# Stationary K/V, bf16 pairs and whole-head transfers in an attention backward pass with one query row

## The chip, the cores and the metric

The kernel runs on one core of a Trainium2 chip. The metric is device time in microseconds of one execution. Every quoted time is the median over the runs of a kernel; where a single run was taken, this is said. The experiments were run in five sessions, each on another chip; the kernel before was run in each of them on the same chip and stayed between 1480.9 and 1481.6 us (medians), so the experiments can be compared with each other.

Names used below: PE is the matmul engine (TensorE), PEld its weight loads, which overlap with PE, DVE the vector engine, ACT the scalar engine, POOL the engine that issues the loads and SP the one that issues the stores. PEclk is the granted clock of PE, where 1.00 is full speed. A "head" is one of 64 (batch, head) pairs.

## The reference

```python
B, H, Sq, Sk, D = 2, 32, 1, 8192, 128          # all bf16

def _fwd_reference(q, k, v):
    scale = q.shape[-1] ** -0.5
    scores = jnp.einsum("bhqd,bhkd->bhqk", q, k) * scale
    p = _softmax(scores, axis=-1)
    return jnp.einsum("bhqk,bhkd->bhqd", p, v)

def reference(q, k, v, grad_out):
    # ... jax.vjp of the forward ...
    return (out, dq, dk, dv)
```

With one query row, a head needs two passes of products over K and V. The scores `q.K` and `dp = do.V` contract over D. The sums `o = p.V` and `dq = ds.K` contract over the 8192 positions. The gradients `dK = ds x q` and `dV = p x do` are outer products. K and V are 2 MB each for a head, and so are dK and dV. Over all heads that makes 268 MB in and 268 MB out, so the transfers are a bound of their own.

## The kernel before

Per head, cut. The partition axis holds 128 groups of 64 consecutive positions (`NT = 64`), so a tile of K is 128 positions by 128 dimensions.

```python
# loads: four pieces of 512 KB each for K and for V (4 KB runs), from POOL
load_eng.dma_start(out=kt[:], in_=k_v[bh, :, c * lp : (c + 1) * lp, :])

# scores and dp: 16 transposes on PE, eviction by ACT, 16 matmuls of one column
for c in range(nch):                                   # 4 chunks
    for which, (Tn, col) in enumerate(((Kn, qcol), (Vn, docol))):
        tp = ps_tp.tile([P, ch, P], BF16, tag="tp")    # 2 buffers
        for i in range(ch):
            nc.tensor.transpose(tp[:, i, :], Tn(n), ident_bf[:])
        ev = evp.tile([P, ch, P], BF16, tag="ev")
        nc.scalar.copy(out=ev[:], in_=tp[:])
        for i in range(ch):
            nc.tensor.matmul(sdp[:, which, n:n+1], lhsT=ev[:, i, :], rhs=col, start=True, stop=True)

# softmax chain: max, exp (E_f), sums, ds ... on DVE, ACT and PE        [cut]

# o, then dq: p (or ds) stationary with one column, V (or K) moving with 128
for n in range(NT):
    nc.tensor.matmul(acc[:, 0, :], lhsT=E_bf[:, n:n+1], rhs=Vn(n), ...)
for n in range(NT):
    nc.tensor.matmul(acc[:, 1, :], lhsT=dS_bf[:, n:n+1], rhs=Kn(n), ...)
nc.scalar.activation(out=orow[:], in_=acc[:, 0, :], func=ACT.Copy, scale=rl[0:1, :])
nc.scalar.activation(out=qrow[:], in_=acc[:, 1, :], func=ACT.Copy, scale=rls[0:1, :])

# outer products on DVE, bf16 times fp32, 16 tiles at a time, stored by SP (4 KB runs)
nc.vector.tensor_tensor(out=dKc[:], in0=qb_b, in1=dSs[...].to_broadcast([P, oc, D]), op=ALU.mult)
```

## Time and profile before

| | before |
|---|---|
| median of 4 runs | 1481.06 us (1480.61 to 1482.01) |
| mean granted clock of PE | 0.978 |
| one head, median (exponentials to exponentials) | 22.4 us |
| ACT busy + ACT waiting | 981.7 + 481 = 1463 of 1480.5 us |
| DMA, mean over the span | 368 GB/s |

These are lines of the page of the kernel before: the span, the busy time of each engine (with its share of the span and its instructions), and the granted clock in tenths over 40 equal slices.

```profile
span 1480.5 us, 54950 instructions
PE 1285.7 (87%) x24898; PEld 1184.9 (80%) x24898; DVE 1260.1 (85%) x1347; ACT 981.7 (66%) x769; POOL 271.9 (18%) x520
PEclk9999999999999999999999999999999999999997
```

PE and DVE both look full, and DMA, at 368 GB/s, is not far away. Busy shares do not say which of them bounds the kernel. The groups of the same page say more. Their columns are: line, engine, operation, output<-input by name, then by shape, the count; after the bar the busy time and the mean ns of one; after the second bar the idle time just before them and what ended most of it.

```profile
L143 ACT COPY ev<-tp 128x2048 bf16<-128x2048 bf16 x512 | 921.4, 1888 | 47.2 <-PE tp L141 46.6
L268 DVE TENSOR_TENSOR dVc<-dob_all,Pn 128x2048 bf16<-128x2048 bf16 x256 | 585.8, 2288 | 0.1
L141 PE MATMUL tp<-ident_bf,kt 128*128 128x128 bf16 x4096 | 302.4, 224 | 9.1 <-DMA kt<-in_k_dram 9.1
L141 PE MATMUL tp<-ident_bf,vt 128*128 128x128 bf16 x4096 | 301.3, 223 | 1.9 <-DMA vt<-in_v_dram 1.9
L245 ACT ACTIVATE orow<-acc,rl 1x128 bf16<-1x128 f32 x64 | 23.1, 360 | 406.7 <-PE acc L237 406.7
L229 PE MATMUL acc<-vt,E_bf 128*1 128x128 bf16 x4096 | 240.9, 220 | 0.0
```

ACT gives the best account of the time, although it is busy for only 66% of it. Its busy time of 981.7 us, its wait of 406.7 us for the accumulation (the line L245), 46.6 us for transposes and 27.9 us for the softmax sum to 1463 of 1480.5 us. So a head is eight evictions in a row, and then a stop. The timeline shows the stop. Its columns are the start in us, the duration, the engine, and what ran; the bracket is the idle time before it.

```profile
712.08 0.32 ACT L169 ACTIVATE E_f<-sdpw,negm 128x64 f32<-128x64 f32 x1 [0.41 <-DVE negm L164]
...
713.20 3.73 PE L229 MATMUL acc<-vt,E_bf 128*1 128x128 bf16 x64
...
716.18 0.19 DVE L217 CAST dS_bf<-dSu 128x64 bf16<-128x64 f32 x1
...
716.77 3.74 PE L237 MATMUL acc<-kt,dS_bf 128*1 128x128 bf16 x64
...
720.54 0.36 ACT L245 ACTIVATE orow<-acc,rl 1x128 bf16<-1x128 f32 x1 [6.30 <-PE acc L237]
```

PE takes 7.5 us for the two accumulations, and ACT idles 6.30 us before it can copy their result. o needs only the exponentials (E_f at 712.08), so it starts 1.1 us after them, and the making of ds, which ends at 716.37, is hidden behind o's 3.73 us.

### The profile page before, as it was taken

The page shows a single profiled execution, that of the slowest core. Times are in us where ns is not written, and L with a number is a line of the kernel's source. Part 1 is how long each engine was busy: PE and PEld are TensorE (multiplying, and loading weights), DVE is VectorE, ACT ScalarE, POOL GpSimd, SP SyncE. Part 2 cuts the span into 40 slices and gives each one's busy share as a digit, 9 for nine tenths or more (in the row PEclk, how much of TensorE's full clock was granted, in tenths as well). Part 3 has the DMA queues.
Part 4 walks back from the last instruction along what each step waited for, and adds up shares of the span by engine and source line. Part 5 has one row for each costly group of instructions (what it writes and reads, how often), then busy time and mean ns, then how long its engine had stood idle before and what let it go on. Part 6 is the DMA issues. An engine that isn't in the chain of part 4 may idle for free. (4 is left out here: it accounts for less than half of the span.)

```text
span 1480.5 us, 54950 instructions
## 1 busy us (share of the span) xinstructions
PE 1285.7 (87%) x24898; PEld 1184.9 (80%) x24898; DVE 1260.1 (85%) x1347; ACT 981.7 (66%) x769; POOL 271.9 (18%) x520
## 2 busy tenths in 40 slices
PE   5898888898988988988889889888888898888894
PEld 5887887887878878878878888788788788888884
DVE  1988988889889889888898898898888888988988
ACT  5667667667576676676675766766766757667663
POOL 3221211211212212112112112122121121121200
PEclk9999999999999999999999999999999999999997
DMA  9999999999999999999999999999999999999954
GB/s 379 415 385 388 370 373 388 354 382 375 358 392 371 357 393 359 372 383 365 383 385 357 387 367 372 389 361 371 389 358 379 386 360 383 368 373 388 363 241 199
DMA packets 148394, 544.70 MB, mean 368 GB/s; under 512 B 16832, under 2 KB 16832, under 8 KB 147904
## 3 DMA queue, kind: packets, MB, share of 16 engines
q0 software_dynamic: 73728, 268.47, 49.9%
q1 hardware_dynamic: 74064, 268.52, 44.6%
q8 instruction: 194, 3.18, 0.8%
q10 hardware_dynamic: 368, 4.21, 0.7%
q14 instruction: 40, 0.33, 0.1%
HBM read 272.66 MB, written 268.47 MB: 366 GB/s over the span
## 5 line engine op out<-in xcount | busy, mean ns | idle before, releaser
L143 ACT COPY ev<-tp 128x2048 bf16<-128x2048 bf16 x512 | 921.4, 1888 | 47.2 <-PE tp L141 46.6
L268 DVE TENSOR_TENSOR dVc<-dob_all,Pn 128x2048 bf16<-128x2048 bf16 x256 | 585.8, 2288 | 0.1
L260 DVE TENSOR_TENSOR dKc<-qb_all,dSs 128x2048 bf16<-128x2048 bf16 x256 | 575.0, 2290 | 0.0
L146 PEld LDWEIGHTS <-ev 128*128 128x128 bf16 x8192 | 243.0, 96 | 236.2 <-ACT ev L143 226.7
L119 POOL DMA_DIRECT2D vt<-in_v_dram x256 | 135.7, 530 | 962.4 <-PE acc L229 943.4
L141 PE MATMUL tp<-ident_bf,kt 128*128 128x128 bf16 x4096 | 302.4, 224 | 9.1 <-DMA kt<-in_k_dram 9.1
L141 PE MATMUL tp<-ident_bf,vt 128*128 128x128 bf16 x4096 | 301.3, 223 | 1.9 <-DMA vt<-in_v_dram 1.9
L245 ACT ACTIVATE orow<-acc,rl 1x128 bf16<-1x128 f32 x64 | 23.1, 360 | 406.7 <-PE acc L237 406.7
L141 PEld LDWEIGHTS <-kt 128*128 128x128 bf16 x4096 | 250.7, 101 | 9.7 <-DMA kt<-in_k_dram 9.7
L141 PEld LDWEIGHTS <-vt 128*128 128x128 bf16 x4096 | 249.3, 100 | 3.9 <-DMA vt<-in_v_dram 2.1
L229 PE MATMUL acc<-vt,E_bf 128*1 128x128 bf16 x4096 | 240.9, 220 | 0.0
L237 PE MATMUL acc<-kt,dS_bf 128*1 128x128 bf16 x4096 | 239.1, 219 | 0.0
L146 PE MATMUL sdpw<-qT_all,ev 128*128 128x1 bf16 x4096 | 141.5, 164 | 110.1 <-ACT ev L143 110.1
L229 PEld LDWEIGHTS <-E_bf 128*1 128x1 bf16 x4096 | 228.9, 84 | 4.6
L237 PEld LDWEIGHTS <-dS_bf 128*1 128x1 bf16 x4096 | 230.5, 84 | 0.0
L146 PE MATMUL sdpw<-doT_all,ev 128*128 128x1 bf16 x4096 | 141.6, 164 | 55.3 <-ACT ev L143 55.1
L116 POOL DMA_DIRECT2D kt<-in_k_dram x256 | 135.8, 531 | 164.1 <-PE acc L237 143.3
L156 DVE TENSOR_REDUCE mp<-sdpw 128x1 f32<-128x64 f32 x64 | 14.4, 225 | 102.7 <-PE sdpw L146 102.7
L178 DVE CUSTOM_DVE_ANT_0 junk<-E_f,sdpw 128x64 bf16<-128x64 f32 x64 | 14.2, 222 | 30.4 <-ACT E_f L169 30.4
L169 ACT ACTIVATE E_f<-sdpw,negm 128x64 f32<-128x64 f32 x64 | 20.2, 316 | 28.1 <-DVE negm L164 27.9
L160 DVE TENSOR_REDUCE gm<-sdpw 1x1 f32<-1x128 f32 x64 | 17.8, 278 | 23.4 <-PE sdpw L158 23.4
L164 DVE TENSOR_SCALAR negm<-sdpw 128x1 f32<-128x1 f32 x64 | 10.2, 159 | 30.7 <-PE sdpw L162 30.7
(33 smaller groups left out, 261.5 us busy)
## 6 DMA issues: line engine op xcount, KB each, us to landing
kt<-in_k_dram POOLq DMA_DIRECT2D x256, 512.0 KB, 12.1
vt<-in_v_dram POOLq DMA_DIRECT2D x256, 512.0 KB, 7.9
out_dram<-dVc SPq DMA_DIRECT2D x256, 512.0 KB
out_dram<-dKc SPq DMA_DIRECT2D x256, 512.0 KB
qb_all<-in_q_dram ACTq DMA_DIRECT2D x1, 2048.0 KB
dob_all<-in_grad_out_dram ACTq DMA_DIRECT2D x1, 2048.0 KB
out_dram<-orow SPq DMA_DIRECT2D x64, 0.2 KB
out_dram<-qrow SPq DMA_DIRECT2D x64, 0.2 KB
```

Source lines behind the costliest of these rows:

```text
L116: load_eng.dma_start(out=kt[:], in_=k_v[bh, :, c * lp : (c + 1) * lp, :])
L119: load_eng.dma_start(out=vt[:], in_=v_v[bh, :, c * lp : (c + 1) * lp, :])
L141: nc.tensor.transpose(tp[:, i, :], Tn(n), ident_bf[:])
L143: nc.scalar.copy(out=ev[:], in_=tp[:])
L146: nc.tensor.matmul(sdp[:, which, n : n + 1], lhsT=ev[:, i, :], rhs=col, start=True, stop=True,)
L160: nc.vector.reduce_max(out=gm[:], in_=mT, axis=AX.X)
L169: nc.scalar.activation(out=E_f[:], in_=sdp[:, 0, :], func=ACT.Exp, bias=negm[:], scale=scale, accum_out=ld[:, 0:1],)
L229: nc.tensor.matmul(acc[:, 0, :], lhsT=E_bf[:, n : n + 1], rhs=Vn(n), start=(n == 0), stop=(n == NT - 1),)
L237: nc.tensor.matmul(acc[:, 1, :], lhsT=dS_bf[:, n : n + 1], rhs=Kn(n), start=(n == 0), stop=(n == NT - 1),)
L245: nc.scalar.activation(out=orow[:], in_=acc[:, 0, :], func=ACT.Copy, scale=rl[0:1, :])
L260: nc.vector.tensor_tensor(out=dKc[:], in0=qb_b, in1=dSs[:, n0 : n0 + oc].unsqueeze(2).to_broadcast([P, oc, D]), op=ALU.mult,)
L268: nc.vector.tensor_tensor(out=dVc[:], in0=dob_b, in1=Pn[:, n0 : n0 + oc].unsqueeze(2).to_broadcast([P, oc, D]), op=ALU.mult,)
```

## The change

The intent was threefold. First, K and V become the stationary operand for o and dq, with one moving column, so that an accumulating matmul costs as little as a score matmul (0.55 us for 16). Second, p and ds are stored as bf16 in pairs, so that the outer products on DVE have two bf16 inputs. Third, a whole head is loaded and stored in one transfer with runs of 16 KB, and o and dq are collected on chip and written once at the end. The core of the diff:

```diff
-        for c in range(nlp):
-            kt = kvp.tile([P, lp, D], BF16, tag=f"K{c}")
-            load_eng.dma_start(out=kt[:], in_=k_v[bh, :, c * lp : (c + 1) * lp, :])
+        kt = kvp.tile([P, NT, D], BF16, tag="K")
+        load_eng.dma_start(out=kt[:], in_=k_v[bh])
   [V alike; q and do broadcast by a matmul in place of 4 MB of loads]
-        for c in range(nch):
-            for which, (Tn, col) in enumerate(((Kn, qcol), (Vn, docol))):
+        for w, src in enumerate((kt, vt)):
+            for c in range(NCH):
   [...]
-            Pn = work.tile([P, NT], F32, tag="Pn")
-            nc.vector.tensor_scalar(out=Pn[:], in0=E_f[:], scalar1=rl[:], ...)
+            Pn = work.tile([P, NT, 2], BF16, tag="Pn")
+            nc.vector.tensor_scalar(out=Pn[:], in0=E_f[:].unsqueeze(2).to_broadcast([P, NT, 2]), ...)
   [dSs alike]
-        acc = ps_acc.tile([1, 2, P], F32, tag="acc")
-        for n in range(NT):
-            nc.tensor.matmul(acc[:, 0, :], lhsT=E_bf[:, n : n + 1], rhs=Vn(n), ...)
-        for n in range(NT):
-            nc.tensor.matmul(acc[:, 1, :], lhsT=dS_bf[:, n : n + 1], rhs=Kn(n), ...)
-        nc.scalar.activation(out=orow[:], in_=acc[:, 0, :], ...)
-        nc.scalar.activation(out=qrow[:], in_=acc[:, 1, :], ...)
+        acc = ps_acc.tile([P, 2], F32, tag="acc")
+        for w, (src, col, norm) in enumerate(((kt, dS_bf, rls), (vt, E_bf, rl))):
+            for n in range(NT):
+                nc.tensor.matmul(acc[:, w : w + 1], lhsT=src[:, n, :], rhs=col[:, n : n + 1], ...)
+            nc.scalar.activation(out=oT[:, w, bh : bh + 1], in_=acc[:, w : w + 1],
+                                 func=ACT.Copy, scale=norm[:])
   [...]
-            nc.vector.tensor_tensor(out=dKc[:], in0=qb_b, in1=dSs[...].to_broadcast([P, oc, D]), ...)
-            store_eng.dma_start(out=dk_v[bh, :, n0 : n0 + oc, :], in_=dKc[:])
+            ob = outp.tile([P, NT, D], BF16, tag=f"o{w}")
+            for n0 in range(0, NT, OC):
+                nc.vector.tensor_tensor(out=ob[...] as pairs, in0=qb as pairs, in1=sc as pairs, ...)
+            store_eng.dma_start(out=dst[bh], in_=ob[:])
```

## The prediction

> **What bounds the kernel now.** A loop between PE and ACT, not the DMA queues directly. The page gives PE 1285.7 us, DVE 1260.1 us and ACT 981.7 us of a span of 1480.5 us. The waits view shows almost no wait of a compute engine on a load (about 20 us, all at the start) and none of DVE on an output buffer. It shows ACT waiting 406.7 us (64 times, 6.4 us a head) for the accumulation of dq, and PE waiting about 165 us for ACT's evictions. The timeline around 700 us shows why: one head takes about 22.4 us; eight evictions follow each other every 1.77 us (14.2 us), then PE runs 2 x 64 accumulating matmuls (3.73 us each 64) while ACT stands idle, because its next instruction is the copy of o.
>
> DMA stands close behind. One-microsecond windows show 400 to 430 GB/s while PE and ACT evict, and 220 to 340 in the accumulation, where loads wait for buffers; the first 100 us run at 402 to 418. The mean is 368. So about 415 GB/s looks like the ceiling of this mix, already with 4 KB runs.
>
> **What the change does.**
> 1. K and V stationary with one moving column: 16 such pairs took 0.55 us in the score matmuls, so 128 take an estimated 4 us instead of 7.5 us. All of it lies on the loop: minus 3.5 us a head, some 220 us.
> 2. bf16 pairs: the DVE products have two 2-byte inputs with a contiguous innermost pair. The Trainium skill, page "VectorE: DVE Perf Modes", section "The perf-mode tier table", gives 1224 ns for such a bf16 product of 2048 and 2293 ns for fp32; this trace has 2290 ns with the fp32 scalar, which agrees. Estimate: 8 x 1.22 = 9.8 us instead of 18.3 us a head, DVE from 19.7 to about 13.5 us. DVE leaves the near-critical set, and the softmax chain waits less behind a product (about 1 us a head).
> 3. Whole-head transfers: a quarter as many packets, 4.2 MB of broadcast less. Loads now start only when a whole head's buffer is free, and PE starts a head only when 2 MB of K is in. The last store is 2 MB (about 5 us) instead of 512 KB.
>
> **New balance.** Compute loop: 22.4 - 3.5 - 0.5 to 1 = about 18.5 to 19 us a head. DMA: 8.39 MB a head at 415 to 425 GB/s = 19.7 to 20.2 us. So the bound moves to DMA. The page "DMA: Bandwidth & Descriptors", section "Bandwidth", measured 425 GB/s for a 16 MB load; no run here shows 16 KB runs yet, so I take 418. Up to the last load, DMA moves about 126 x 4.19 = 528 MB: 1264 us; plus a start of 3 us and a tail of about 30 us after the last load (V phase 7, softmax 4.5, products 10, last store 7). That is 1297; with some loss between loop and queues I say 1305 us, range 1255 to 1375. Chance of faster by over 2%: 0.95; within 2%: 0.04; slower: 0.01.
>
> **What would show it right.** Accumulating groups of about 30 ns a pair; DVE products near 1.22 us; DVE busy 850 to 900 us; PE busy lower; ACT's wait for acc about halved; new waits of PE on K and V loads of some us a head, spread over the run; mean 405 to 420 GB/s.
>
> **What would make it wrong.** Products staying at 2.29 us (then DVE bounds: about 1450 us). Larger packets lifting DMA above 430 GB/s or lowering it by read/write mixing. PE waiting for whole-head loads long enough for its clock to fall. Compute slower than 20 us a head because ACT still stops for both accumulations.

## The result, and the profile after

| | before | after |
|---|---|---|
| median | 1481.06 us | 1400.01 us (1397.86 to 1402.66, 4 runs) |
| ratio | | 0.9453 (95%: 0.9439 to 0.9466) |
| mean granted clock | 0.978 | 0.705 |
| one head, median | 22.4 us | 21.4 us |
| DMA, mean | 368 GB/s | 386 GB/s |

A ratio is the mean time of one kernel's fast runs over that of the other's of the same rounds, so it is not quite the ratio of the medians. The gain was 81 us where 176 had been forecast, and the time lies above the predicted range.

The same lines of the page, now of the changed kernel:

```profile
span 1399.4 us, 53434 instructions
PE 1238.2 (88%) x24964; PEld 1138.2 (81%) x24964; DVE 745.6 (53%) x1413; ACT 989.3 (71%) x769; POOL 69.8 (5%) x138
PEclk9667677767676667776777676657776777676565
```

DVE lost 515 us of work, and PE lost only 48. The clock row explains the second: PE ran at six or seven tenths of its full clock in the mean of almost every slice. The groups of the changed kernel:

```profile
L117 ACT COPY ev<-tp 128x2048 bf16<-128x2048 bf16 x512 | 934.7, 1869 | 96.5 <-PE tp L115 94.0
L115 PE MATMUL tp<-ident_bf,vt 128*128 128x128 bf16 x4096 | 452.2, 299 | 7.2 <-issue 7.2
L115 PE MATMUL tp<-ident_bf,kt 128*128 128x128 bf16 x4096 | 367.1, 233 | 6.2 <-DMA kt<-in_k_dram 4.2
L228 DVE TENSOR_TENSOR ob<-qb,Pn 128x2048 bf16<-128x2048 bf16 x256 | 306.7, 1220 | 0.2
L214 PE MATMUL acc<-E_bf,vt 128*128 128x1 bf16 x4096 | 125.4, 166 | 32.1 <-issue 31.7
L221 ACT ACTIVATE oT<-acc,rl 128x1 bf16<-128x1 f32 x64 | 16.9, 263 | 178.1 <-PE acc L214 178.1
L214 PE MATMUL acc<-dS_bf,kt 128*128 128x1 bf16 x4096 | 116.0, 164 | 5.5 <-DVE dS_bf L191 2.6
L221 ACT ACTIVATE oT<-acc,rls 128x1 bf16<-128x1 f32 x64 | 16.9, 264 | 96.6 <-PE acc L214 96.6
```

The accumulations fell as predicted, from 240.9 + 239.1 us to 125.4 + 116.0 us (-239 us), and the products fell from 2288 to 1220 ns each. But the same 8192 transposes grew from 302.4 + 301.3 us to 452.2 + 367.1 us (+216 us), although nothing in them was changed. And ACT still stops for the accumulation, now twice a head: 178.1 + 96.6 = 274.7 us, after 406.7 us. Its whole account reads: busy +8, wait for the accumulation -132, wait for transposes +47, wait for the softmax -5. That is -82 us, and the time fell by 81. So the question is why these two waits stayed so long.

These are windows of one microsecond of the changed kernel around one accumulation. The columns after the length are the busy time of PE, PEld, DVE, ACT and POOL with counts, then the granted clock, the busy share of the DMA engines and GB/s.

```profile
713.00:714.00 1.00, 0.98 (x39) 0.92 (x36) 1.00 (x2) 0.00 (x0) 0.00 (x0) 0.63 0.96 410
714.00:715.00 1.00, 1.00 (x34) 1.00 (x32) 1.00 (x2) 0.26 (x1) 0.41 (x1) 0.50 1.08 459
...
723.00:724.00 1.00, 0.90 (x13) 0.73 (x11) 0.00 (x0) 0.95 (x2) 0.00 (x0) 0.75 1.05 442
```

The accumulation starts at 712.34. In the window from 713 to 714 the clock is halved, and it stays at 0.50 for nine microseconds (714 to 723), of which PE is busy for 8.2 us. It is no lack of work for PE that lowers the clock; what does is counted out below, under the width of the moving operand. And this is the timeline of the same stretch:

```profile
708.87 0.31 ACT L143 ACTIVATE E_f<-sdpw,negm 128x64 f32<-128x64 f32 x1 [0.41 <-DVE negm L138]
...
712.34 1.95 PE L214 MATMUL acc<-dS_bf,kt 128*128 128x1 bf16 x64
...
714.33 0.26 ACT L221 ACTIVATE oT<-acc,rls 128x1 bf16<-128x1 f32 x1 [1.53 <-PE acc L214]
...
714.85 1.89 PE L214 MATMUL acc<-E_bf,vt 128*128 128x1 bf16 x64
...
716.77 1.91 PE L115 MATMUL tp<-ident_bf,vt 128*128 128x128 bf16 x16
716.78 0.26 ACT L221 ACTIVATE oT<-acc,rl 128x1 bf16<-128x1 f32 x1 [2.19 <-PE acc L214]
```

Three things are to be seen. Sixteen transposes take 1.91 us at the half clock, where the kernel before took 1.06 us for them. The accumulation starts 3.5 us after the exponentials, not 1.1, as dq waits for ds. And ACT stands idle for 1.53 and 2.19 us, although each accumulation takes only 1.9 us: it has no transposed tile left to evict while PE accumulates.

One more wait is new. The view of PE's waits gives 31.7 + 9.2 + 3.5 = 44 us to "issue", which means that PE waited for nothing that the profile shows. The kernel before has none of these.

### The profile page after: what moved, and what is told of

The parts are those of the page before. It is cut to its first block, busy times and chain, and to the rows that moved or that the text cites. A ratio compares the mean times of both kernels' runs of the same rounds, so it can differ in the third digit from the quotient of the medians.

```text
span 1399.4 us, 53434 instructions
## 1 busy us (share of the span) xinstructions
PE 1238.2 (88%) x24964; PEld 1138.2 (81%) x24964; DVE 745.6 (53%) x1413; ACT 989.3 (71%) x769; POOL 69.8 (5%) x138
## 3 DMA queue, kind: packets, MB, share of 16 engines
q8 instruction: 195, 3.19, 0.8%
## 4 chain that ended last, share of the span: by engine, by line
PE 59%; ACT 24%; issue 10%; DVE 6%; DMA 1%; POOL 0%; ACTq 0%; POOLq 0%
PE tp L115 28%; ACT ev L117 23%; PE acc L214 16%; PE sdpw L120 11%; PE sdpw L136 1%; PE sdpw L165 1%; ACT oT L221 1%; DVE ob L228 1%; DVE dSu L182 1%; DVE negdelta L169 1%; ACT E_f L143 1%; DVE dS_bf L191 1%; PE sdpw L132 1%; DVE rl L167 1%; DMA kt<-in_k_dram 1%
## 5 line engine op out<-in xcount | busy, mean ns | idle before, releaser
L115 PE MATMUL tp<-ident_bf,vt 128*128 128x128 bf16 x4096 | 452.2, 299 | 7.2 <-issue 7.2
L115 PEld LDWEIGHTS <-vt 128*128 128x128 bf16 x4096 | 397.6, 140 | 9.5 <-issue 9.2
L115 PE MATMUL tp<-ident_bf,kt 128*128 128x128 bf16 x4096 | 367.1, 233 | 6.2 <-DMA kt<-in_k_dram 4.2
L120 PE MATMUL sdpw<-qdT,ev 128*128 128x1 bf16 x8192 | 295.1, 166 | 83.4 <-ACT ev L117 77.0
L228 DVE TENSOR_TENSOR ob<-qb,Pn 128x2048 bf16<-128x2048 bf16 x256 | 306.7, 1220 | 0.2
L228 DVE TENSOR_TENSOR ob<-qb,dSs 128x2048 bf16<-128x2048 bf16 x256 | 296.1, 1221 | 0.0
L115 PEld LDWEIGHTS <-kt 128*128 128x128 bf16 x4096 | 268.7, 104 | 9.4 <-DMA kt<-in_k_dram 5.4
L214 PE MATMUL acc<-E_bf,vt 128*128 128x1 bf16 x4096 | 125.4, 166 | 32.1 <-issue 31.7
L214 PEld LDWEIGHTS <-vt 128*128 128x128 bf16 x4096 | 121.3, 105 | 34.5 <-issue 34.4
L221 ACT ACTIVATE oT<-acc,rl 128x1 bf16<-128x1 f32 x64 | 16.9, 263 | 178.1 <-PE acc L214 178.1
L214 PEld LDWEIGHTS <-kt 128*128 128x128 bf16 x4096 | 116.8, 100 | 11.5 <-issue 11.2
L214 PE MATMUL acc<-dS_bf,kt 128*128 128x1 bf16 x4096 | 116.0, 164 | 5.5 <-DVE dS_bf L191 2.6
L92 POOL DMA_DIRECT2D kt<-in_k_dram x64 | 33.9, 530 | 1095.1 <-PE acc L214 1095.1
L221 ACT ACTIVATE oT<-acc,rls 128x1 bf16<-128x1 f32 x64 | 16.9, 264 | 96.6 <-PE acc L214 96.6
L94 POOL DMA_DIRECT2D vt<-in_v_dram x64 | 33.8, 528 | 156.5 <-PE tp L115 154.6
```

Source lines behind the costliest of these rows:

```text
L92: load_eng.dma_start(out=kt[:], in_=k_v[bh])
L94: load_eng.dma_start(out=vt[:], in_=v_v[bh])
L115: nc.tensor.transpose(tp[:, i, :], src[:, c * CH + i, :], ident_bf[:])
L120: nc.tensor.matmul(sdp[:, w, n : n + 1], lhsT=ev[:, i, :], rhs=qdT[:, w, bh : bh + 1], start=True, stop=True,)
L214: nc.tensor.matmul(acc[:, w : w + 1], lhsT=src[:, n, :], rhs=col[:, n : n + 1], start=(n == 0), stop=(n == NT - 1),)
L221: nc.scalar.activation(out=oT[:, w, bh : bh + 1], in_=acc[:, w : w + 1], func=ACT.Copy, scale=norm[:])
```

## The experiments

The theories at the start were these. Theory A: the halved clock is the cause; the time it costs PE is the missing gain. Theory B: DMA bounds already. Theory C: the two stops of ACT and the order of the accumulations are the cause. A' and A'' are later forms that join A and C, and a text that gives a letter another sense says which. Theory D came up later for the "issue" waits: PE's own instructions come late. "Changed kernel" below is the kernel after the change.

### Width of the moving operand: 64 columns, and 16

```diff
-        acc = ps_acc.tile([P, 2], F32, tag="acc")
+        acc = ps_acc.tile([P, 2, 64], F32, tag="acc")
-                    rhs=col[:, n : n + 1],
+                    rhs=col[:, n : n + 1].to_broadcast([P, 64]),
```

The same column is moved 64 times, and 63 of the results are thrown away.

> The changed kernel with each of the 128 accumulating matmuls a head moving the same column 64 times (step 0) instead of once; results unchanged. Theory A (128 matmuls of one moving column in a row make the PE's granted clock fall to half, and the half clock makes the transposes after them slow): mean granted clock back above 0.95 from 0.71, transposes of V 0.22 us mean again instead of 0.30, time 1290 to 1330 us. Theory B (the DMA queues bound the changed kernel at about 390 to 400 GB/s and the clock does not matter): the clock may rise, the time stays within 1% of 1400 us. Theory C (the loop is set by ACT stopping for both accumulations, not by the clock): time stays within 2% of 1400 us with the clock up.

Measured: 1362.03 us, ratio 0.9185 (0.9164 to 0.9207). The clock row of its page, and its groups of transposes:

```profile
PEclk9999999999899989999989889999999889989997
L115 PE MATMUL tp<-ident_bf,kt 128*128 128x128 bf16 x4096 | 333.9, 224 | 7.9 <-issue 4.0
L115 PE MATMUL tp<-ident_bf,vt 128*128 128x128 bf16 x4096 | 298.1, 230 | 8.3 <-issue 8.1
```

The mean clock is back at 0.949, and the transposes at 333.9 + 298.1 us, 187 us less than in the changed kernel. The accumulations got dearer, 144.2 + 148.4 us. So more work for the matmul array made the kernel faster. But the time went only 38 us of the 95 us to the prediction, and the expectation of theory A was missed. ACT's wait for the accumulation even rose to 314.6 us, while its wait for transposes fell from 94.0 to 31.0 us. The clock is a cause, not the whole one. The time lies outside the ranges of all three theories, as 1362 us is 2.7% under 1400.

The run with 16 columns (the same edit with 16) came later, to see how wide is wide enough.

> The changed kernel with each accumulating matmul moving 16 columns of the same value in place of one (64 columns gave a clock of 0.95, one column 0.71). If the clock follows the share of time in which the array has columns to work on: the mean granted clock lies between, 0.75 to 0.90, and the time between 1362 and 1400 us, about 1375 to 1390. Rival (it is a threshold, and 16 columns are enough): 0.93 to 0.95 and 1358 to 1366 us.

Measured: 1398.01 us, ratio 0.9443 (0.9429 to 0.9457), clock 0.739. That is below the range expected for a clock that follows the width in proportion, and far below the rival's: 16 columns are hardly better than one (0.705 and 1400.01 us). No width between 16 and 64 was run.

The kept traces show what the clock follows. This is a count over them, made afterwards, and not a run of its own. In the traces of the 18 kernels that compute the clock is 1.00 or 0.50 and changes only in steps of 3.41 us. Count for each step the columns that the matmuls starting in it move: 128 for a transpose, 64 for a wide accumulation, 1 for a score matmul. There are 7151 steps, without those at either end of a run. After each of the 1579 steps with fewer than 2750 columns the next step had half the clock, and after 4371 of the 4375 steps with 3250 or more it had the full clock, whatever the clock was before; in between both occur. These are the steps of the changed kernel around the accumulation shown above:

| step, us | PE busy, us | columns moved | clock in it | clock in the next |
|---|---|---|---|---|
| 706.43 to 709.84 | 2.97 | 3236 | 1.00 | 1.00 |
| 709.84 to 713.25 | 2.87 | 2487 | 1.00 | 0.50 |
| 713.25 to 716.67 | 3.40 | 747 | 0.50 | 0.50 |
| 716.67 to 720.08 | 2.61 | 2064 | 0.50 | 0.50 |
| 720.08 to 723.49 | 3.41 | 3728 | 0.50 | 1.00 |

So it is not PE's busy time that counts: in the third step PE is busy almost throughout and moves few columns. The mean is 2716 columns a step with one column, 3028 with 16 and 4120 with 64; in the kernel before, whose accumulation moves 128, it is 4991. Sixteen columns leave the mean between the two limits, and 64 lift it over them.

### The old accumulation in the changed kernel

```diff
-                    acc[:, w : w + 1], lhsT=src[:, n, :], rhs=col[:, n : n + 1],
+                    acc[:, w, :],      lhsT=col[:, n : n + 1], rhs=src[:, n, :],
   [row copies and small stores as before; dq still first, ACT still stops twice]
```

> The changed kernel with the accumulation of before (p and ds stationary, K and V moving 128 columns, row copies and small stores of o and dq), everything else as changed. Theory A: clock above 0.95; each accumulation again 3.7 us instead of 1.9, transposes fast again; the two nearly cancel, so 1370 to 1430 us, that is, K and V stationary earned almost nothing by itself. Theory B: 1400 us, as the queues bound. Theory C (ACT stops for the accumulations): about 3.7 us a head longer than the changed kernel, 1600 us or more, or back to 1480.

Measured: 1557.19 us, ratio 1.0509 (1.0491 to 1.0526), clock 0.926. No expectation was met; theory C, with about 1600 us, came nearest. ACT waits 476.9 us for the accumulation, 70 us more than in the kernel before, and the time is 76 us more. So inside the changed kernel the stationary K and V are worth 157 us (1557 to 1400), and the rest of the change, with the old accumulation, loses 76 us against the kernel before; that makes the 81 us. ACT's account puts 70 of the 76 us on the wait for the accumulation. The new order and the second stop are the likely reason; the run with o first, below, shows for the one-column form that the order costs time.

### Where ACT stops: the copies on DVE, and both edits together

```diff
-            nc.scalar.activation(out=oT[...], in_=acc[:, w : w + 1], func=ACT.Copy, scale=norm[:])
+            nc.vector.tensor_scalar(out=oT[...], in0=acc[:, w : w + 1], scalar1=norm[:],
+                                    scalar2=None, op0=ALU.mult)
```

> The changed kernel with only the two scaled copies of o and dq a head moved from ACT to DVE (which is 53% busy); the matmuls stay one column wide. Theory A' (ACT is the loop, and its two stops for the accumulations, 275 us, are the largest loss; the low clock is the second): ACT's wait for the accumulation goes to zero, but PE at the low clock (mean about 0.7) cannot feed ACT, whose wait for transposes grows well above 94 us: 1330 to 1380 us. Rival (clock alone): no gain, 1390 to 1400 us. Rival (stops alone): 1290 to 1310 us, the queues' floor, whatever the clock.

Measured: 1368.96 us, ratio 0.9242 (0.9225 to 0.9258), clock 0.733. ACT no longer waits for the accumulation at all, and still waits: 354.7 us for transposes, after 94.0 us. Most of the wait changed its name. The copy on ACT was not what kept ACT idle; PE accumulates while ACT has nothing to evict.

The next kernel has both the 64 columns and the copies on DVE.

> Both: accumulating matmuls 64 columns wide and the two copies on DVE. Theory A': both losses gone, the loop falls to about 18 us a head, under the queues' 19.4 us (8.39 MB at the 432 GB/s of the 16 KB copy), so PE now waits for loads and the time is 1256 us plus a tail of some 30 us: 1280 to 1320 us. Rival (something else holds the loop at 20.5 us): 1345 to 1362 us.

Measured: 1357.4 us, ratio 0.9166 (0.9127 to 0.9205), clock 0.938. Here the first theory fell and the rival was right: with the clock up and no copy on ACT the kernel still waits, 349.1 us for transposes. In the head around 715 us ACT has two such gaps of 2.44 and 2.61 us, and they fall into the two accumulations.

### The order: o before dq

```diff
-        for w, (src, col, norm) in enumerate(((kt, dS_bf, rls), (vt, E_bf, rl))):
+        for w, src, col, norm in ((1, vt, E_bf, rl), (0, kt, dS_bf, rls)):
```

> The changed kernel with only the order of the two accumulations changed back to that of before, o (which needs only exp) ahead of dq (which needs ds, ready some 3 us later). Theory A': the first accumulation no longer waits behind the softmax chain, ACT's stops shrink by 1 to 2 us a head, 1300 to 1370 us unless the clock falls further. Rival (the order does not matter): 1400 us within 1%.

Measured: 1369.18 us, ratio 0.923 (0.921 to 0.9251), clock 0.704. Swapping the two groups is worth 31 us with the clock just as low. ACT's wait for the accumulation falls from 274.7 to 155.4 us, and its wait for transposes rises from 94.0 to 175.7 us.

### One part alone in the kernel before

Stationary K and V alone, with one column, and everything else as before:

```diff
-                acc[:, 0, :], lhsT=E_bf[:, n : n + 1], rhs=Vn(n),
+                acc[:, 0:1],  lhsT=Vn(n), rhs=E_bf[:, n : n + 1],
   [dq alike; the columns are collected and turned at the end]
```

> The kernel before with only the accumulation changed (K and V stationary, o and dq as columns, gathered at the end): one part alone, with fp32 scalars for the products and 4 KB runs. Its instruction order shifts somewhat with it. Theory A': clock falls to 0.7 to 0.8 as in the changed kernel, and with DVE at 2.29 us a product (about 21 us of DVE work a head) the gain is small: 1400 to 1480 us. Rival (narrow matmuls do not lower the clock by themselves): clock above 0.95.

Measured: 1569.39 us, ratio 1.0572 (1.053 to 1.0614), clock 0.607. The clock row of its page:

```profile
PEclk9878575766555555555555555555555555555555
```

The part that was worth 157 us in the changed kernel costs 88 us in the kernel before. After the first third the clock stays at one half in every slice. The time lies outside both expectations. The scheduler also ordered the instructions differently here: after the last head's exponentials the run goes on for 81.6 us, where the kernel before needs 23.9, and in most of it DVE alone works off products that had been left over. This difference of 58 us is the larger part of the 88. So this run shows that the part can lose, and not how much of the loss is the clock's.

The bf16 pairs alone:

```diff
-            Pn = work.tile([P, NT], F32, tag="Pn")
+            Pn = work.tile([P, NT, 2], BF16, tag="Pn")
   [dSs alike; the products read both inputs as pairs]
```

> The kernel before with only the products changed to bf16 pairs. In its trace ds was ready 0.7 us before the accumulation of o ended, so the softmax chain hides behind that accumulation: DVE falls from 1260 to about 800 us busy, and the time hardly moves, 1462 to 1481 us (my theory: DVE was never on the loop). Rival (DVE at 85% was close enough to hold the loop): 1400 to 1450 us.

Measured: 1475.74 us, ratio 0.9963 (0.9949 to 0.9978). DVE's busy time fell from 1260.1 to 718.0 us, and ACT waits 406.8 us for the accumulation, where it waited 406.7 us.

So 542 us of DVE work were removed for 5 us of time. DVE was 85% busy and still not on the loop, and hardly any wait of the softmax behind a product was there to be saved. In the changed kernel, where dq waits for the softmax chain, the pairs were not tested by themselves.

### The transfers by themselves

These two kernels only load and store, in the sizes of the changed kernel and of the kernel before. Their outputs are wrong, which doesn't matter for the times.

```diff
-        [everything between the loads and the stores]
+        store_eng.dma_start(out=dst[bh], in_=...)      # nothing is computed
```

> Wrong result on purpose: only the loads and stores of the changed kernel (16 KB runs, whole heads, K stored as dk and V as dv), no computing. Theory A: 537 MB at 415 to 430 GB/s, 1250 to 1300 us, so 1400 us is not the queues' floor. Theory B: 1370 to 1400 us.

> Wrong result on purpose: the same copy with the transfers of the kernel before (512 KB, 4 KB runs). If run length matters to the queues, several per cent slower than the 16 KB copy; my guess is 1280 to 1320 us, 1 to 2% slower than it. In any case well below the 1481 us of the kernel before.

Measured, one run each, so their state is unknown: 1255.98 us with runs of 16 KB (432 GB/s in the steady part) and 1301.5 us with runs of 4 KB (420 GB/s). So theory B fell: the transfers would have allowed 144 us less than the changed kernel took. The copy with 4 KB runs took 3.6% longer than the other, where 1 to 2% had been expected. They also show that the third part of the change has a value, 45 us, that can be had only by a compute loop which is faster than that.

### Accumulation spread over the next head

If PE accumulates while ACT has nothing to evict, the accumulation has to be cut up and put between transposes. This kernel cuts it in six slices of 21 or 22 matmuls and runs them between the chunks of the next head, o first, 64 columns wide, with the copies on DVE; the transposes run one chunk ahead.

```diff
+        ev = turn(0)                                   # 16 transposes + eviction
+        for g in range(2 * NCH):
+            nxt = turn(g + 1) if g + 1 < 2 * NCH else None
+            if prev is not None and g < 6:
+                acc_slice(prev, g)                     # 21 or 22 matmuls of the head before
+            [16 score matmuls on ev]
+            ev = nxt
```

> The changed kernel with the 128 accumulating matmuls of a head cut into six pieces of 21 or 22 that PE runs between the transposes of the next head's first six chunks (order pinned, o ahead of dq), 64 columns wide, both copies on DVE at the end. Theory A'' (what held the earlier fixes at 1357 us is that PE runs a whole accumulation while ACT has nothing to evict, whoever copies the result): ACT's wait for transposes falls from 350 us to under 120, PE starts to wait for loads, and the time reaches the queues' floor plus a tail, 1280 to 1320 us. Rival (another limit, for instance queues that give only 400 GB/s beside the computing): 1340 to 1362 us.

Measured: 1339.34 us, ratio 0.9039 (0.9014 to 0.9064), clock 0.897. It is faster than all the others up to here, and slower than the theory expected, just outside the rival's range too. ACT's wait for transposes, expected under 120 us, fell only from 349.1 to 264.9 us. The view of PE's waits shows a new cost (us in total, times, longest):

```profile
PE tp L140 <- issue: 52.3, 36, 2.9
PE sdpw L153 <- issue: 48.4, 36, 2.9
PE acc L101 <- issue: 35.4, 29, 2.3
PE tp L140 <- DMA kt<-in_k_dram: 25.8, 21, 4.1
```

PE waits 136 us in all for nothing that the profile shows, after 44 us in the changed kernel.

The same kernel with one column in place of 64 asks whether the clock still falls when the narrow matmuls come in short slices between transposes.

```diff
-                rhs=col[:, n : n + 1].to_broadcast([P, 64]),
+                rhs=col[:, n : n + 1],
```

> As the pipelined kernel, but one column wide. Theory A (the clock falls when narrow matmuls fill some microseconds in a row, not by their number): spread among transposes they leave the clock above 0.9 and the time within 1.5% of the pipelined wide kernel. Rival (the number of narrow matmuls in any place lowers the clock): clock 0.65 to 0.8 and 1340 to 1400 us.

Measured: 1355.11 us, ratio 0.9144 (0.9122 to 0.9166), clock 0.664, PE 93% busy. The rival was right: the clock falls all the same. By the count of columns that had to be so, for spreading the matmuls does not add columns: the mean is 2797 a step. One column in place of 64 costs 16 us here.

### PE's waits for nothing: run length, traffic and position

The changed kernel with 64 columns, with runs of 4 KB in place of 16 KB:

```diff
-        load_eng.dma_start(out=kt[:], in_=k_v[bh])
+        for c in range(4):
+            load_eng.dma_start(out=kt[:, c * 16 : (c + 1) * 16, :], in_=k_v[bh, :, c * 16 : (c + 1) * 16, :])
   [V and the stores alike]
```

> The kernel of the wide accumulation (1362 us) with loads and stores cut into 512 KB pieces of 4 KB runs, buffers still whole heads. Theory D (PE's waits that the profile calls issue, some 45 us of PE in it and 44 in the changed kernel and near 0 in the kernel before, are instruction fetch that queues behind 16 KB packets): those waits fall below 10 us and the time falls by 10 to 40 us, to 1320 to 1352. Rival (run length does not touch PE, only the queues' ceiling, 420 against 432 GB/s): issue waits as they were, 1355 to 1375 us.

Measured: 1358.95 us, ratio 0.9175 (0.9161 to 0.9188). These waits fell from 29.2 + 12.1 + 2.1 = 43 us to 8.9 + 3.7 + 1.6 = 14 us, and the time stayed the same within the noise. The waits fell as theory D said, if not below 10 us; the time is the rival's.

The pipelined kernel with runs of 4 KB and of 8 KB (the same edit):

> The pipelined kernel with runs of 4 KB in place of 16 KB, nothing else. Theory D (PE's waits with nothing to wait for in the records, 136 us in the pipelined kernel, are its instructions being fetched behind long packets on the same DMA engines): these waits fall well under 136 us, to 20 to 60 us, and the time to 1310 to 1335 us, held there by the transfers (the bare 4 KB transfers took 1301.5 us). Rival (the waits belong to the pipelined order of instructions, not to the transfers): they stay above 100 us and the time at or above 1340 us.

> The pipelined kernel with runs of 8 KB. Theory D: PE's waits with nothing to wait for lie between those of 16 KB runs (136 us) and of 4 KB runs of the same order, 60 to 110 us, and the time between 1315 and 1340 us. Rival: the waits are 136 us, within 15, and the time is 1335 to 1345 us.

Measured: with 4 KB the waits are 16.4 + 11.2 + 8.0 = 36 us and the time is 1363.96 us (ratio 0.9209, 0.9194 to 0.9224); with 8 KB they are 21.8 + 18.1 + 13.5 = 53 us and the time is 1339.28 us (0.9038, 0.9025 to 0.9052). The waits shrink with the run length, as theory D said; with 8 KB they ended a little under the expected range. The time at 4 KB is the rival's, and the time at 8 KB lies in both ranges and tells nothing. What PE won it lost again, for it now waits 115.7 us for K loads (100.2 us with 8 KB, 25.8 us with 16 KB).

What these waits are is told by their position. This is a stretch of PE's timeline in the pipelined kernel, between two of them:

```profile
710.17 0.57 PE L101 MATMUL acc<-dS_bf,kt 128*128 128x64 bf16 x13 [0.71 <-issue]
710.58 0.54 PE L153 MATMUL sdpw<-qdT,ev 128*128 128x1 bf16 x16
710.98 1.05 PE L140 MATMUL tp<-ident_bf,vt 128*128 128x128 bf16 x16
711.87 0.81 PE L101 MATMUL acc<-dS_bf,kt 128*128 128x64 bf16 x21
712.52 0.54 PE L153 MATMUL sdpw<-qdT,ev 128*128 128x1 bf16 x16
712.92 1.05 PE L140 MATMUL tp<-ident_bf,vt 128*128 128x128 bf16 x16
714.04 0.55 PE L153 MATMUL sdpw<-qdT,ev 128*128 128x1 bf16 x16
714.55 0.95 PE L140 MATMUL tp<-ident_bf,kt 128*128 128x128 bf16 x14
716.38 0.28 PE L140 MATMUL tp<-ident_bf,kt 128*128 128x128 bf16 x2 [0.87 <-issue]
```

The counts from the first wait to the second add up to 13 + 16 + 16 + 21 + 16 + 16 + 16 + 14 = 128 matmuls. Counted over the whole traces of four kernels (the changed one, and the pipelined one with 16 KB, with 4 KB and with less traffic), nearly all distances between such waits are multiples of 128, give or take a few that the counting at the borders of windows adds. With its weight load each matmul is two instructions, so 128 matmuls are 256 instructions. The Trainium skill, page "Runtime: NRT & Kernel Launch", section "Instruction fetch mechanics", says that an engine's instructions are refilled in blocks of 16 KiB, or 256 instructions, while the block before is executed. Traces agree: the queue called "instruction" has 195 packets with 3.19 MB (16.4 KB each) for 24964 matmuls, which is one per 128. The packets of this queue confirm it: in the traces of the 18 kernels that compute, 819 of 827 such waits end 1.0 to 1.8 us after one of them has landed. So PE waits at block boundaries for its next instructions. The same section calls this cost mostly hidden; here it is up to 136 of 1338 us.

What makes a block late is settled less well. Two runs took the load off the transfers by storing dv only for the last head, so they give a wrong result.

```diff
-            store_eng.dma_start(out=dst[bh], in_=ob[:])
+            if w == 0 or bh == BH - 1:
+                store_eng.dma_start(out=dst[bh], in_=ob[:])
```

> The pipelined kernel with dv stored for the last head only, so wrong on purpose: a quarter or so of the traffic is gone and the DMA engines have room. Theory D: PE's waits with nothing to wait for fall under 20 us in all, and the time shows the pace of the compute loop alone, some 18 to 19 us a head, 1150 to 1230 us. Rival (the waits come with the order of instructions): they stay about 100 us or more and the time falls little, to 1290 us or above.

> The pipelined kernel with 4 KB runs and dv stored for the last head only, so wrong on purpose. PE's waits that the profile puts down to nothing come at multiples of 128 matmuls, so they are instruction fetches; with three quarters of the traffic and 16 KB runs they still took 109 us of 1253. If it is the length of the packets ahead of a fetch that makes it late: under 25 us here, and the time is the compute loop's own, 1150 to 1200 us. Rival (it is something else than the packets, and the 4 KB runs only hid it behind waits for loads): 80 us or more, and 1230 us or above.

Measured, one run each, their state unknown: 1253.3 us with 16 KB, and these waits are still 41.9 + 37.8 + 28.5 = 108 us; 1224.14 us with 4 KB, and they are still 34.4 + 32.1 + 20.8 = 87 us, against the 36 us of the same kernel with all its traffic. Both times lie between the two expectations; the waits are the rival's in both runs. So theory D in the form "full engines and long packets delay the fetch" does not hold: with 4 KB runs and less traffic the waits more than doubled. In that run PE waits hardly for anything else, and in the run with all its traffic it waits 115.7 us for K loads.

The kept traces say more, though no run was made for it: what counts first is how fast PE uses up a block. In the changed kernel 62 blocks were used up in less than 6 us, and after 45 of these the next one was late; of the 130 others only 3. In the kernel before, with the pairs alone, and in the changed kernel with the old accumulation, no block was used up in less than 6 us, and PE has no such wait. The last of these has runs of 16 KB, so long packets alone do not make a block late. They do add to it: in the pipelined kernel with all its traffic the next block was late after 90 of 112 such short blocks with 16 KB runs, and after 39 of 96 with 4 KB. With less traffic it was 72 of 129 and 69 of 132. Why the run length counts in one case and not in the other stays open.

What these two runs do give is the pace of the compute loop with room in the transfers. The exponentials of three consecutive heads in the second run:

```profile
600.75 0.31 ACT L179 ACTIVATE E_f<-sdpw,negm 128x64 f32<-128x64 f32 x1 [0.65 <-DVE negm L174]
619.76 0.31 ACT L179 ACTIVATE E_f<-sdpw,negm 128x64 f32<-128x64 f32 x1 [2.52 <-DVE negm L174]
638.27 0.31 ACT L179 ACTIVATE E_f<-sdpw,negm 128x64 f32<-128x64 f32 x1 [1.16 <-DVE negm L174]
```

That is 19.0 and 18.5 us a head; the mean over all heads is 18.7 us, and 19.1 us in the first of the two runs.

### Earlier loads for the pipelined kernel

The pipelined kernel with 8 KB runs, a fourth buffer for K, and half-head output tiles (three of each):

```diff
-        kt = kvp.tile([P, NT, D], BF16, tag="K")
+        kt = kvp.tile([P, NT, D], BF16, tag="K", bufs=4)
   [output tiles of half a head, stored as soon as they are full]
```

> The pipelined kernel with 8 KB runs, a fourth buffer for K, and output tiles of half a head, three of each, stored as soon as they are full. The run without the fourth buffer had PE wait 100 us for K loads. If these loads are late only because they are issued late (when a K buffer comes free): PE's wait for loads falls under 30 us and the time to 1300 to 1322 us. Rival (the transfers as a whole are full, and a load issued earlier lands later): PE still waits 60 us or more and the time is 1328 to 1342 us.

Measured: 1335.14 us (1334.54 to 1336.79), ratio 0.9018 (0.9003 to 0.9033). This is the fastest correct kernel, by a margin over the run without the fourth buffer (1339.28 us) that is near the noise. PE's wait for K loads fell from 100.2 to 1.1 us, as the first theory said; the time stayed where the rival put it. The waits moved on:

```profile
DVE ob L254 <- DMA out_dram<-ob: 266.9, 67, 6.3
PE qbp L125 <- DVE qb L133: 65.4, 44, 4.0
```

DVE now waits for its stores to leave, and PE behind it. PE's waits for instructions rose from 53 to 81 us. K loads land after 35.4 us in the median, where they took 24.6 us without the fourth buffer. A load issued earlier only landed later. That fits transfers which are full as a whole, at 406 GB/s in the mean and about 420 in the first third of the span; it is not shown, as no run has bare transfers of 8 KB runs beside it.

## Why the prediction was wrong

**What held.** The loop between PE and ACT bounded the kernel before. The accumulation costs what was estimated: 64 pairs in 1.9 us, 30 ns a pair. The product costs 1220 ns, as the Trainium skill has it (page "VectorE: DVE Perf Modes", section "The perf-mode tier table": 1224 ns for bf16, 2293 ns for fp32); the traces have 1220 and 2288 to 2290 ns, so they agree. The direction was right, and so was the ceiling of the transfers, though a little low: 432 GB/s measured for 16 KB runs, where 418 had been taken. DVE's busy time fell further than forecast, to 745.6 us where 850 to 900 had been expected.

**The step that failed** is the sentence "Compute loop: 22.4 - 3.5 - 0.5 to 1 = about 18.5 to 19 us a head." The loop took 21.4 us, 1.0 us less than before where 4 to 4.5 had been summed up. So the bound did not move to DMA, and the mean rate was 386 GB/s and not 405 to 420. Three terms of this sum were wrong.

1. *"All of it lies on the loop: minus 3.5 us a head."* PE did save 239 us in the accumulations. It gave 216 us back in the transposes, for with one column the steps of the clock move too few columns to keep it full. The prediction had named a falling clock as a risk, but for another reason, waiting for loads; PE was 88% busy and its wait for loads was 4.2 us, once. The runs with 64 columns show what the clock is worth, less the dearer accumulation: 38 us in the changed kernel, 16 us in the pipelined one.
2. *The same term, on the side of ACT.* A saving on PE shortens the loop only as far as ACT's stop gets shorter. This stop fell from 406.7 to 274.7 us, not to about half. The changed kernel begins with dq, which has to wait for ds, and stops ACT twice. Order alone is worth 31 us, and moving both copies away from ACT another such 31 us, each measured by itself on the changed kernel; the gains overlap and do not add up (64 columns and DVE copies together give 43 us, where 38 and 31 were had singly). As the last line of its section on risks the prediction had "because ACT still stops for both accumulations". That came true, but the sum had no term for it.
3. *"The softmax chain waits less behind a product (about 1 us a head)."* In the kernel before, the bf16 pairs alone gave 5 us in the whole run, under 0.1 us a head. DVE had not been on the loop, for all its 85%.

A fourth loss was in no term of the sum: PE's instruction blocks come late, 44 us of waits in the changed kernel and none before. How much time these 44 us cost was not isolated; in the changed kernel with 64 columns their fall from 43 to 14 us moved the time by nothing that can be told from noise.

**Was the sum itself possible?** Yes, but by a different kernel. A loop of 18.5 to 19 us a head was reached by the pipelined kernel with 64 columns when it had room in the transfers. With all the traffic, the best version took 1335 us, with DVE waiting 266.9 us for stores. The predicted 1305 us needed both at once.

**What stays open**: why an instruction block takes as long as it does to arrive, and when the run length counts for it; how much time the late blocks cost; which width between 16 and 64 columns is enough; what the whole-head transfers do alone in the kernel before, which was not run; and how much of the loss of the stationary form alone in the kernel before is due to the clock and how much to the other order.

## What to carry to other kernels

Cost a change on PE with its effect on the granted clock: a matmul that loads a full 128x128 stationary operand for a single moving column is cheap by itself and slowed the transposes around it. In these traces the clock followed the columns moved in each 3.41 us and not PE's busy time, and padding the moving operand to 64 columns, which is more work, made the kernel 38 us faster. When one engine feeds another, count what the receiving engine can do meanwhile: the stationary form cut PE's accumulations by 239 us and the time of the changed kernel by 157 us, and ACT still stood idle for 275 us, as it had nothing to evict meanwhile; with wide columns and DVE copies, cutting the block into slices between transposes took another 18 us (1357 to 1339 us). A high busy share, like DVE's 85%, is no sign that the engine lies on the loop; sum up one engine's busy time and waits until they make the span, and spend the effort where its waits end.

## What the Trainium skill lacked or had wrong

- Page "TensorE: Matmul & The Clock Gate", section "Part 1: The HAM clock gate": it explains the half clock by how busy PE has been, with idle windows of about 3.4 us as the cause. The steps of 3.41 us agree with that length. But here a step in which PE was busy for 3.40 us was followed by half the clock, as it moved 747 columns. What the clock followed was the columns moved in a step: half after all 1579 steps with fewer than 2750, full after 4371 of 4375 with 3250 or more. The mean clock was 0.61 to 0.74 in every kernel with 1 or 16 columns, and 0.85 to 0.95 in those with 64 columns. That narrow matmuls can keep PE busy and still lose the clock is lacking.
- The same page, section "Part 4: PE-mode transpose", says that full clock does not engage for transposes. Here it does: all 960 steps that moved 3250 or more columns by transposes, and fewer than 150 by other matmuls, were followed by the full clock; none of the 1058 such steps with fewer than 2750 was.
- Page "Runtime: NRT & Kernel Launch", section "Instruction fetch mechanics": the block of 256 instructions agrees with these traces, but "mostly hidden" does not: PE waited 44 us of 1399 us in the changed kernel and 136 us of 1338 us in the pipelined one, in waits that the profile puts down to nothing. How such waits look in a profile is lacking, and so is that they come when PE uses up a block fast: late after 45 of 62 blocks of under 6 us in the changed kernel, and after 3 of the 130 others.
- Page "DMA: Bandwidth & Descriptors", section "Bandwidth", has 425 GB/s for a 16 MB load alone. Loads and stores mixed reached 432 GB/s with runs of 16 KB and 420 GB/s with runs of 4 KB; the page has no figure for the mix by run length.
